# Queue orders from a list scheduler in a fused attention and feed-forward kernel

## The chip, the cores and the metric

The kernel runs on one core of a Trainium2 chip. The metric is the time of one execution on the device in microseconds, as the median of several runs.

## What is computed

Attention over 8 batches, 8 heads, 576 positions and head dimension 64, with a relative-position bias, and then a feed-forward layer over the 4608 rows of 512 that come out of it. Cut to what matters:

```python
scores = matmul(q, k.T) / sqrt(64)                 # 8 x 8 x 576 x 576
n = abs(i - j)                                     # distance of positions
bucket = n if n < 16 else min(31, 16 + int(log(n / 16) / log(8) * 15))
scores += bias_table[bucket, head]                 # constant for n >= 128
attn = exp(scores - max); attn /= attn.sum(-1)
x = matmul(attn, v)                                # as 4608 x 512, heads side by side
h = x @ w_in                                       # 512 -> 2048
out = maximum(0.01 * h, h) @ w_out                 # 2048 -> 512, float32
```

The inputs are float32; the kernel works in bf16 with float32 sums.

## The kernel before

**Attention.** The work is cut into 32 pairs of heads, pair n being batch n // 4 and heads 2p and 2p + 1. For each pair DVE copies the pair's rows of q and k into `pr` (L256), which are transposed to `qt` and `kt`: on PE (L272) with copies out of PSUM (L286, L291) for pairs 0 to 9, by a DMA transpose (L264) from pair 10 on. `apart` (L278) multiplies the last 64 columns with a mask `own`, so that both heads share one matmul there. `qk_mm` (L301 to L309) makes the scores in six chunks, keys along the partitions, into a PSUM pool of two buffers; ACT takes the exponential of each chunk into `at` and `at4` (L319, L321, L326), of which there are two sets, taken in turn. `band` (L347) multiplies the part near the diagonal by the exponentials of the bias, relative to the constant far value, which drops out in the normalization. `av` (L360, L362) makes the product with v for one head (25 matmuls into `ps_o`, one buffer); a column of ones in v gives the sums, and DVE normalizes into `opair` (L365, L366). `x_transposes` brings the pair into `xT`, on PE (L384) with a copy (L385) for pairs 0 to 5 and 31, by DMA (L377) for the others.

**The band factors.** One row of exponentials per head, `ub`, is made by ACT from the transposed table (L183) and by DVE's copies of runs of equal buckets (L186 to L194), stored to a tensor `u_row` in memory (L200), and read back with a shift of one element per partition as `hk` (L202, heads 0 and 1 first) and, for the last 64 keys, `hk4` (L209, `hk_101` in the profile).

**Feed-forward.** Nine tiles of 512 rows. First layer: 16 pieces of 4 matmuls (L396), each followed by ACT's leaky ReLU into `gt` (two buffers). Second layer: 4 row blocks of 16 matmuls (L407), in pieces of 4, each block copied by DVE and stored by SP. All PSUM tiles of these pieces, and of PE transposes, share a pool of three buffers.

**Loads.** q, k, v and the weights are read as float32 and cast on the way, all issued on POOL's queue (software DMA): q and k in `load_qk` (L111), v in L119 to L146, the weights in L232 and L238, in the order of the program.

**What sets the order.** The program is written in the order in which each engine is to run it; every engine takes its own instructions in that order and waits for semaphores. A loop over the pairs holds, for pair n, scores and exponentials in three groups of two chunks, the two AV halves of pair n - 1 between them, the transposes of pair n + 1, and eight slots for feed-forward pieces, alternately of the first and of the second layer:

```python
        moe(1)
        if live:
            exp_band(n, 1, ps_b)
        if n > 0:
            av(n - 1, 0)
        if n + 1 < N:
            transpose_q(n + 1)
```

A piece is taken if its inputs are there by the program's order: a tile of the first layer needs all four pairs of the last batch that it reads, and a tile of the second layer begins only while a tile of the first layer is under way, apart from the end. Junk matmuls (`spin`, L459; 27 of them) fill PE's waits at the start. In batch 0 the band products of pair 0 stand behind its last exponential.

Of the kernel before, what the change touches and what calls it, by code (L numbers as in the profile page):

```python
# [35 lines left out]

@with_exitstack
def kernel(
# [32 lines left out]
    qt_pool = ctx.enter_context(tc.tile_pool(name="qt", bufs=2))  # L71
# [13 lines left out]
    nc.scalar.activation(warm, warm, AF.Exp)  # L85
# [14 lines left out]
    kts_ = [per.tile([P, S + P], BF16, name=f"kt{i}") for i in range(2)]  # L100
# [56 lines left out]
    def clear_edges(eng, i):  # L157
        eng.memset(at_[i][:, ATW : ATW + SL], 1.0)
        eng.memset(at4_[i][:, S : S + SL], 1.0)

    junk = per.tile([P, 512], BF16, name="junk")
    nc.vector.memset(junk, 0.0)
    clear_v(nc.vector, 0)
    clear_edges(nc.vector, 0)
# [3 lines left out]
    tabT = per.tile([H, NB], FP32, name="tabT")  # L168
    with nc.allow_non_contiguous_dma(reason="a table of 256 numbers"):
        nc.sync.dma_start(out=tabT, in_=bias_table.rearrange("u h -> h u"))  # L170
    load_qk(0, 0, 2)
    make_identity(nc, ident)

    e8 = per.tile([H, NB], BF16, name="e8")
    UW = 4 * P
    BW = 3 * P
    ub = per.tile([H, UW], BF16, name="ub")
    nc.vector.memset(ub, 1.0)  # L180
    negc = per.tile([H, 1], FP32, name="negc")
    nc.vector.tensor_scalar(negc, tabT[:, NB - 1 : NB], -1.0, None, op0=ALU.mult)
    nc.scalar.activation(e8, tabT, AF.Exp, bias=negc[:, 0:1], scale=1.0)  # L183
    C0 = 2 * P - 1
    small = NB // 2
    nc.vector.tensor_copy(out=ub[:, C0 : C0 + small], in_=e8[:, 0:small])  # L186
    for u, lo, hi in bucket_runs(NB, BAND, S):
        if lo >= small:
            nc.vector.tensor_copy(
                out=ub[:, C0 + lo : C0 + hi + 1],  # L190
                in_=e8[:, u : u + 1].to_broadcast([H, hi - lo + 1]),
            )
    row = ub[:, :]
    nc.vector.tensor_copy(  # L194
        out=ub[:, C0 - BAND + 1 : C0],
        in_=bass.AP(tensor=row.tensor, offset=row.offset + C0 + BAND - 1,
                    ap=[list(row.ap[0]), [-1, BAND - 1]]),
    )
    udr = nc.dram_tensor("u_row", [H, UW], BF16, kind="Internal")
    nc.sync.dma_start(out=udr.ap(), in_=ub)  # L200
# [6 lines left out]
    load_hk(0, 2)  # L207
    for e in range(2):
        nc.sync.dma_start(  # L209
            out=hk4[e * SL : (e + 1) * SL, :, :],  # L210
            in_=bass.AP(tensor=udr, offset=e * UW + SL + P, ap=[[1, SL], [2 * UW, n_pairs], [1, P + SL]]),
        )
    load_hk(2, H)
# [8 lines left out]

    load_qk(0, 2, H)
    clear_edges(nc.vector, 1)
    load_v(0, 0, 2, True)
    load_v(0, 2, H, False)
    clear_v(nc.gpsimd, 1)
    load_qk(1, 0, H)
# [16 lines left out]
    qts, kts, ops_ = {}, {}, {}  # L245
    N = len(items)
    AHEAD = 3

    prs, turned = {}, {}

    def pair_rows(n):

        b, p = items[n]
        t = prs[n] = pr_pool.tile([RQ, 2, NC, 2 * D], BF16, name="pr")
        for j, src in enumerate((qn, kn)):
            nc.vector.tensor_copy(out=t[:, j, :, :].rearrange("r c (e d) -> r c e d", e=2),  # L256
                                  in_=src[b % NBUF][0:RQ, 2 * p : 2 * p + 2, :, :].rearrange("r e c d -> r c e d"))

    def by_dma(n):
        return n >= 2 * n_pairs + 2  # L260

# [4 lines left out]
    def turned_pair(n, j):  # L266

        if by_dma(n):
            return turned[n][:, j * NC : (j + 1) * NC, :].rearrange("p c r -> p r c")
        ps = ps_m_pool.tile([P, 8 * P], BF16, name="ps_t", tag="m")  # L270
        for c in range(NC):
            nc.tensor.transpose(ps[:, c * RQ : (c + 1) * RQ], in_=prs[n][0:RQ, j, c, :],  # L272
                                identity=ident[0:RQ, 0:RQ])
        return ps[:, 0:S].rearrange("p (c r) -> p r c", c=NC)

    def apart(t):

        nc.vector.tensor_tensor(  # L278
            out=t[:, S : S + P].rearrange("p (e i) -> p e i", e=2),
            in0=t[:, NJ * P : S].unsqueeze(1).to_broadcast([P, 2, SL]),  # L280
            in1=own, op=ALU.mult)

    def transpose_q(n):
        qt = qts[n] = qt_pool.tile([P, S + P], BF16, name="qt")
        copy = nc.scalar.copy if 0 < n < n_pairs else nc.vector.tensor_copy
        copy(out=qt[:, 0:S].rearrange("p (r c) -> p r c", c=NC), in_=turned_pair(n, 0))  # L286
        apart(qt)

    def transpose_k(n):
        kt = kts[n] = kts_[n % 2]  # L290
        nc.vector.tensor_copy(out=kt[:, 0:S].rearrange("p (r c) -> p r c", c=NC), in_=turned_pair(n, 1))  # L291
        apart(kt)

    def qk_mm(n, u):

        qt, kt = qts[n], kts[n]
        ps = ps_s_pool.tile([P, 2, 512], FP32, name="ps_s")
# [12 lines left out]
        return ps  # L310

    def at_view(n):
        return at_[n % 2][:, 0:ATW].rearrange("p (e c i) -> p e c i", e=2, c=NJ)

    def exp_band(n, u, ps):
        b, p = items[n]
        at, at4 = at_view(n), at4_[n % 2]
# [9 lines left out]
        if n > 0:  # L327
            band(n, u)
        elif u == NJ + 1:
            for j in range(NJ + 2):  # L330
                band(n, j)

    def band(n, u):
        b, p = items[n]
        at, at4 = at_view(n), at4_[n % 2]
        hp = hk[:, 2 * p : 2 * p + 2, :]
        if u == 0:
            o, m = at[:, :, 0, 0 : 2 * P], mirrored(hp, P, 3 * P)
        elif u in (1, 2):
            o, m = at[:, :, u, (u - 1) * P : (u + 2) * P], mirrored(hp, 0, 3 * P)  # L340
        elif u == NJ:
            o, m = at[:, :, 3, 2 * P : S], mirrored(hp, 0, S - 2 * P)
        elif u == NJ + 1:
            o, m = at4[:, 3 * P : S], mirrored(hk4[:, p, :], 0, P + SL)
        else:
            return
        nc.vector.tensor_tensor(out=o, in0=o, in1=m, op=ALU.mult)  # L347

    def av(n, e):
        b, p = items[n]  # L350
        i = b % NBUF
        at, at4 = at_[n % 2], at4_[n % 2]
        if e == 0:
            ops_[n] = op_pool.tile([P, NJ + 1, 2 * D], BF16, name="opair")
        opair = ops_[n]
        ps = ps_o_pool.tile([P, NJ + 1, D + 1], FP32, name="ps_o", tag="ps_o")
        for ic in range(NJ + 1):
            for c in range(NJ):
# [4 lines left out]
                             start=False, stop=True)  # L363
        rcp = rc_pool.tile([P, NJ + 1, 1], FP32, name="rcp")
        nc.vector.reciprocal(rcp, ps[:, :, D : D + 1])  # L365
        nc.vector.tensor_tensor(out=opair[:, :, e * D : (e + 1) * D], in0=ps[:, :, 0:D],  # L366
                                in1=rcp.to_broadcast([P, NJ + 1, D]), op=ALU.mult)

    def x_by_dma(n):
        return n_pairs + 2 <= n < N - 1  # L370

    def x_transposes(n):
        b, p = items[n]
        opair = ops_[n]
        w = (NJ + 1) * P
        if x_by_dma(n):
            nc.sync.dma_start_transpose(  # L377
                out=xT[p][:, b * S : b * S + w].rearrange("p (i t) -> p i t", t=P),
                in_=opair.rearrange("p i d -> p (i d)"),
            )  # L380
            return
        ps = ps_m_pool.tile([P, 8 * P], BF16, name="ps_tx", tag="m")
        for ic in range(NJ + 1):
            nc.tensor.transpose(ps[:, ic * P : (ic + 1) * P], in_=opair[:, ic, :], identity=ident)  # L384
        nc.vector.tensor_copy(out=xT[p][:, b * S : (b + 1) * S], in_=ps[:, 0:S])  # L385


    gts = {}

    def ffn_in(T):  # L390
        t0 = T * TT
        gt = gts[T] = gt_pool.tile([P, n_fc, TT], BF16, name="gt")
        for f in range(n_fc):
            pm = ps_m_pool.tile([P, TT], FP32, name="pm1", tag="m")
            for c in range(n_cc):
                nc.tensor.matmul(pm, lhsT=w_in_sb[:, c, f * P : (f + 1) * P], rhs=xT[c][:, t0 : t0 + TT],  # L396
                                 start=(c == 0), stop=(c == n_cc - 1))
            nc.scalar.activation(gt[:, f, :], pm, AF.Prelu, bias=0.0, scale=1.0, alpha=0.01)  # L398
            yield

    def ffn_out(T):
        t0 = T * TT
        gt = gts.pop(T)
        for ts in range(TT // P):
            pm = ps_m_pool.tile([P, DM], FP32, name="pm2", tag="m")
            for f in range(n_fc):
                nc.tensor.matmul(pm, lhsT=gt[:, f, ts * P : (ts + 1) * P], rhs=w_out_sb[:, f, :],  # L407
                                 start=(f == 0), stop=(f == n_fc - 1))
                if f % 4 == 3 and f < n_fc - 1:
                    yield  # L410
# [33 lines left out]
    def moe_rest():  # L444
        while piece("in", True) | piece("out", True):
            pass
# [110 lines left out]
```

## Time and profile before

| | us |
|---|---|
| three runs | 399.03, 397.37, 397.79 |
| median | 397.79 |
| span of the profiled execution, first to last instruction | 396.8 |
| PE busy / ACT busy / DVE busy / POOL busy in it | 372.0 / 247.9 / 203.7 / 66.7 |

The profile is of one execution; for it only the span is given, no separate time, and what lies around the span is in the runs' times alone. Times in its rows count from the start of the span. Busy times of PE overlap from one matmul to the next, so the starts of matmuls tell the rate.

### The profile page before, as it was taken

What the parts mean: (1) busy time and instruction counts of PE and PEld (TensorE: products, weight loads), DVE (VectorE), ACT (ScalarE), POOL (GpSimd) and SP (SyncE); (2) the same over time, 40 slices, a digit from 0 to 9 for tenths busy, and PEclk for the clock granted to TensorE, in tenths of its full rate; (3) what the DMA queues carried; (4) which work ended last, traced back from release to release, by engine and by line L of the source; (5) the groups of instructions that cost most, each with busy time, mean ns of one, the idle gap of its engine ahead of it and who ended that gap; (6) DMA issues with size and microseconds to landing.
All of it is one profiled execution on the core that took longest, in us unless ns stands there. A gap on an engine that the chain in (4) does not pass through costs nothing.

```text
span 396.8 us, 8116 instructions
## 1 busy us (share of the span) xinstructions
PE 372.0 (94%) x3328; PEld 189.9 (48%) x3382; DVE 203.7 (51%) x552; ACT 247.9 (62%) x342; POOL 66.7 (17%) x96
## 2 busy tenths in 40 slices
PE   7678798889999999999999999999999999999995
PEld 3355455444445555554455545554454544444442
DVE  6479778665566666665555665555554310101021
ACT  2677788877777777777777777777777333333300
POOL 8733520340051004200330022000000000000000
PEclk9979999999999999999999999999999999999999
DMA  8999999499279935992599349333111110101112
GB/s 109 194 206 187 203 185 133 64 170 149 68 82 142 165 74 78 158 158 69 64 162 150 70 82 126 74 74 74 43 45 45 43 55 26 55 27 41 40 53 79
DMA packets 103549, 39.89 MB, mean 101 GB/s; under 512 B 82512, under 2 KB 97880, under 8 KB 103512
## 3 DMA queue, kind: packets, MB, share of 16 engines
q0 software_dynamic: 53600, 18.36, 44.6%
q1 hardware_dynamic: 49912, 21.02, 26.2%
q8 instruction: 26, 0.43, 0.5%
q14 instruction: 11, 0.09, 0.1%
HBM read 37.68 MB, written 9.45 MB: 119 GB/s over the span
## 4 chain that ended last, share of the span: by engine, by line
PE 82%; ACT 5%; DVE 5%; DMA 3%; issue 3%; SPq 0%; ACTq 0%; DVEq 0%
PE ps_o L360 8%; PE ps_s L301 7%; ACT at_114 L319 2%; PE ps_o L362 2%; DMA hk<-u_row 2%; ACT at_113 L319 2%; PE ps_s L308 2%; PE ps_s L305 1%; DMA u_row<-ub 1%; DVE opair L366 1%; ACT gt L398 1%; PE pm_4269 L407 1%; PE pm_2498 L407 1%; PE pm_4886 L407 1%; PE pm_3385 L407 1%
## 5 line engine op out<-in xcount | busy, mean ns | idle before, releaser
L396 PEld LDWEIGHTS <-w_in_sb 128*128 128x128 bf16 x576 | 50.1, 98 | 71.9 <-issue 20.1
L407 PEld LDWEIGHTS <-gt 128*128 128x128 bf16 x576 | 53.2, 98 | 56.9
L319 ACT ACTIVATE at_113<-ps_s 128x1024 bf16<-128x1024 f32 x64 | 64.5, 1023 | 17.2 <-PE ps_s L301 16.9
L319 ACT ACTIVATE at_114<-ps_s 128x1024 bf16<-128x1024 f32 x64 | 64.3, 1023 | 11.5 <-PE ps_s L301 11.5
L347 DVE TENSOR_TENSOR at_113<-at_113,hk 128x512 bf16<-128x512 bf16 (+1 forms) x64 | 32.0, 504 | 42.9 <-ACT at_113 L319 40.4
L347 DVE TENSOR_TENSOR at_114<-at_114,hk 128x512 bf16<-128x512 bf16 (+1 forms) x64 | 32.2, 505 | 42.5 <-ACT at_114 L319 41.3
L360 PEld LDWEIGHTS <-at_113 128*128 128x128 bf16 x640 | 27.8, 99 | 13.8 <-DVE opair L366 7.5
L366 DVE TENSOR_TENSOR opair<-ps_o,rcp 128x320 bf16<-128x320 f32 x64 | 31.5, 491 | 2.2
L360 PEld LDWEIGHTS <-at_114 128*128 128x128 bf16 x640 | 27.2, 98 | 9.8 <-DVE opair L366 5.1
L119 POOL DMA_DIRECT2D vn_107<-in_v_dram x12 | 10.6, 897 | 83.3 <-PE ps_o L362 83.3
L301 PE MATMUL ps_s<-qt,kt_111 64*128 64x512 bf16 x128 | 20.9, 389 | 2.7 <-ACT at_114 L319 1.0
L119 POOL DMA_DIRECT2D vn_106<-in_v_dram x12 | 10.8, 911 | 69.2 <-PE ps_o L362 62.7
L301 PE MATMUL ps_s<-qt,kt_110 64*128 64x512 bf16 x128 | 20.3, 382 | 2.0 <-ACT at_113 L319 1.1
L360 PE MATMUL ps_o<-vn_106,at_113 128*128 128x65 bf16 x320 | 15.5, 197 | 4.8 <-DVE opair L366 3.2
L360 PE MATMUL ps_o<-vn_106,at_114 128*128 128x65 bf16 x320 | 14.4, 194 | 1.7 <-DVE opair L366 1.7
L362 PEld LDWEIGHTS <-at_0_115 128*128 128x128 bf16 x160 | 15.7, 98 | 0.0
L362 PEld LDWEIGHTS <-at_1_116 128*128 128x128 bf16 x160 | 15.6, 97 | 0.0
L365 DVE RECIPROCAL rcp<-ps_o 128x5 f32<-128x5 f32 x64 | 12.1, 189 | 6.1 <-PE ps_o L362 6.1
L321 ACT ACTIVATE at_114<-ps_s 128x512 bf16<-128x512 f32 x16 | 9.6, 598 | 8.6 <-PE ps_s L305 8.6
L360 PE MATMUL ps_o<-vn_107,at_113 128*128 128x65 bf16 x320 | 14.3, 193 | 0.1
L360 PE MATMUL ps_o<-vn_107,at_114 128*128 128x65 bf16 x320 | 14.3, 194 | 0.0
L286 DVE COPY qt<-tu 128x576 bf16<-128x576 bf16 x22 | 14.3, 648 | 0.0
(849 smaller groups left out, 760.9 us busy)
## 6 DMA issues: line engine op xcount, KB each, us to landing
out_dram<-y SPq DMA_DIRECT2D x36, 256.0 KB, 2.2
w_in_sb<-in_moe_w_in_dram POOLq DMA_DIRECT2D x2, 1024.0 KB, 13.8
vn_107<-in_v_dram POOLq DMA_DIRECT2D x16, 128.0 KB, 5.2
w_out_sb<-in_moe_w_out_dram POOLq DMA_DIRECT2D x2, 1024.0 KB, 14.2
qn_102<-in_q_dram POOLq DMA_DIRECT2D x6, 288.0 KB, 10.4
kn_104<-in_k_dram POOLq DMA_DIRECT2D x6, 288.0 KB, 10.6
qn_103<-in_q_dram POOLq DMA_DIRECT2D x6, 288.0 KB, 10.6
kn_105<-in_k_dram POOLq DMA_DIRECT2D x6, 288.0 KB, 11.2
```

Source lines behind the costliest of these rows:

```text
L119: nc.gpsimd.dma_start(out=vn[i][:, c, :, 0:D], in_=v[b, :, c * P : (c + 1) * P, :].rearrange("h s d -> s h d"),)
L286: copy(out=qt[:, 0:S].rearrange("p (r c) -> p r c", c=NC), in_=turned_pair(n, 0))
L301: nc.tensor.matmul(ps[:, e, :], lhsT=kt[r, u * P : (u + 1) * P], rhs=qt[r, 0:512], start=True, stop=True)
L319: nc.scalar.activation(at[:, :, u, 0:512], ps, AF.Exp, scale=scale)
L321: nc.scalar.activation(at[:, :, :, 512:S].rearrange("p e c i -> p c e i"), ps[:, 0, :].rearrange("p (c e i) -> p c e i", e=2, i=SL), AF.Ex ...
L347: nc.vector.tensor_tensor(out=o, in0=o, in1=m, op=ALU.mult)
L360: nc.tensor.matmul(ps[:, ic, :], lhsT=at[:, o : o + P], rhs=vn[i][:, c, 2 * p + e, :], start=(c == 0), stop=False)
L362: nc.tensor.matmul(ps[:, ic, :], lhsT=at4[:, ic * P : (ic + 1) * P], rhs=v4[i][:, p, e, :], start=False, stop=True)
L365: nc.vector.reciprocal(rcp, ps[:, :, D : D + 1])
L366: nc.vector.tensor_tensor(out=opair[:, :, e * D : (e + 1) * D], in0=ps[:, :, 0:D], in1=rcp.to_broadcast([P, NJ + 1, D]), op=ALU.mult)
L396: nc.tensor.matmul(pm, lhsT=w_in_sb[:, c, f * P : (f + 1) * P], rhs=xT[c][:, t0 : t0 + TT], start=(c == 0), stop=(c == n_cc - 1))
L407: nc.tensor.matmul(pm, lhsT=gt[:, f, ts * P : (ts + 1) * P], rhs=w_out_sb[:, f, :], start=(f == 0), stop=(f == n_fc - 1))
```

## The change

The loop is replaced by a plan. Each step of the program becomes a task with an engine, a cost in us that is written into the code, the tasks it comes after, the PSUM buffers it takes and gives back, and a rank. At build time `Plan.order` simulates the engines: again and again it takes the task that can start first, ties going to the lower rank, and the program is emitted in that order. Attention has ranks 10 n, feed-forward 10000 and up, so a feed-forward piece is taken where no attention task is ready. Batch 0's scores get rank 10 n - 25 and come ahead of AV. Loads have landing times written in. From pair 8 on, scores also wait for a first-layer piece (`PACE`, `LEAD`), so that attention does not run too far ahead. Junk matmuls fill the planned waits of PE ahead of the first feed-forward piece; they are again 27.

Other edits: `qt` and `kt` have three buffers instead of two; pair 2's exponentials go to a third attention buffer, which lies in the second `gt` buffer until tile 1 needs it. q and k of pair 0 are read as float32 without a cast on SP's and ACT's queues into the first `gt` buffer (`raw`), and cast by DVE (q) and ACT (k) in the row copies; all of batch 0's v likewise by six DMAs on ACT's queue, cast by POOL. The band row is a matmul of the exponentials of the table (32 buckets x 8 heads) with a one-hot matrix `hot` that DVE builds from the identity; one DVE copy brings it to `ub`. The order of the read-backs is now hk of heads 0 and 1, hk of heads 2 to 7, hk4. POOL's loads are held by `gate`, a one-element copy that waits: the last q and k load of batch 0 until `ub` exists, the first half of `w_in` until hk of heads 2 to 7 has landed. Behind it follow q and k of batch 1 (first half), the second half of `w_in`, v of batch 1, the rest of q and k, and `w_out`. The masks for v and the edges are cleared by POOL. Products with `own` of pairs 1 and 2 go to POOL; the copies into `qt` of pairs 0 to 2 and 4, and into `kt` of pair 4, to ACT. Pair 0's band products come as soon as the factors are there. In batch 0 the second AV half uses a buffer of the shared pool in place of `ps_o`. Pair 7's output is transposed by PE, not by DMA. The second layer of a tile may begin whenever its first layer is complete.

```diff
+class Plan:
...
+    def order(self):
...
+                for t in ts:
+                    if any(d["end"] is None for d in t["after"] + t["behind"]):
+                        continue
+                    r = now
+                    for d in t["after"]:
+                        r = max(r, d["end"] + (self.LAG if d["engine"] != e else 0.0))
+                    for k in set(t["take"]):
+                        s, m = sorted(self.slots[k]), t["take"].count(k)
+                        r = max(r, s[m - 1]) if len(s) >= m else None
...
+                    key = (r, t["rank"], t["n"])
+                    if pick is None or key < pick[0]:
+                        pick = (key, t, r)
...
-    qt_pool = ctx.enter_context(tc.tile_pool(name="qt", bufs=2))
+    qt_pool = ctx.enter_context(tc.tile_pool(name="qt", bufs=3))
...
+    nc.sync.dma_start(out=raw[:, 0, :, :], in_=q[0, 0:2, :, :].rearrange("h (r c) d -> r h (c d)", c=NC))
+    nc.scalar.dma_start(out=raw[:, 1, :, :], in_=k[0, 0:2, :, :].rearrange("h (r c) d -> r h (c d)", c=NC))
+    nc.sync.dma_start(out=tab[:, 0, :], in_=bias_table)
...
+    load_qk(0, 2, 4)
+    load_qk(0, 4, 6)
...
+    def spread_table():
+        ps = outs["u"] = ps_o_pool.tile([P, 512], FP32, name="ps_u", tag="ps_o")
+        nc.tensor.matmul(ps[0:H, :], lhsT=e8, rhs=hot, start=True, stop=True)
...
+    def load_v_raw():
+        for c in range(NJ):
+            nc.scalar.dma_start(out=vraw_sb[:, c, :, :], in_=v[0, :, c * P : (c + 1) * P, :].rearrange("h s d -> s h d"))
+        for e in range(2):
+            nc.scalar.dma_start(out=vraw4[e * SL : (e + 1) * SL, :, :],
+                                in_=v[0, e::2, NJ * P : S, :].rearrange("h s d -> s h d"))
...
+    def gate(t):
+        nc.gpsimd.tensor_copy(out=w_in_sb[0:1, 0, 0:1], in_=t)
...
+    plan = Plan({"S": 2, "O": 1, "M": 2})
...
+    e8t = add("ACT", 0.25, [sh], exp_table, -1)
+    spr = add("PE", 0.4, [e8t], spread_table, -1, take=["O"])
+    cpu = add("DVE", 0.6, [spr], copy_u_row, -1, give=["O"])
+    urt = add("SP", 0.1, [cpu], store_u_row, -1, tail=2.6)
+    hkt = add("SP", 0.1, [urt], lambda: load_hk(0, 2), -1, tail=2.8)
+    hkr = add("SP", 0.1, [urt], lambda: (load_hk(2, H), load_hk4()), 1, tail=5.5)
...
+    pool_load(("qk", 0, 2), 1.6, lambda: (gate(ub[0:1, 0:1]), load_qk(0, 6, H)), after=[cpu], land=17.0)
+    vrt = add("ACT", 0.6, [], load_v_raw, 5, tail=9.0)
+    vc = [add("POOL", 0.7, [vrt], lambda c=c: cast_v(c), 0) for c in range(NJ + 1)]
...
+            t = add("PE", 0.3 * len(us), ds + before + order_s[-1:],
+                    lambda us=us: [score(n, u) for u in us], rank + (-25 if n < n_pairs else 2), take=["S"] * len(us))
...
+        for e in range(2):
+            k = "M" if b == 0 and e == 1 else "O"
+            avs.append(add("PE", 0.78, done, lambda e=e: av(n, e), soon + 4, take=[k]))
+            nms.append(add("DVE", 0.68, [avs[-1]] + old + nms, lambda e=e: norm(n, e), soon + 3, give=[k]))
...
-    for n in range(N + 1):
...
-    moe_rest()
+    spin(9)
+    plan.run(spin)
```

In the order that results, PE's queue for batch 0 is: junk, the one-hot matmul, the transposes of pair 0, then scores of pair 0 and 1 with the transposes of pairs 1 and 2; the first AV half of pair 0 stands between score chunks 2 and 3 of pair 1, its second half between chunks 3 and 4. The first feed-forward piece stands behind score chunk 1 of pair 4, and the second layer of tile 0 begins among the pairs of batch 1. From batch 2 on each pair has eight feed-forward pieces, as before.

More of the change, by code (lines that the diff above doesn't have):

```diff
@@ L182 @@
[L182 to L198, printed above, removed]
-    udr = nc.dram_tensor("u_row", [H, UW], BF16, kind="Internal")
-    nc.sync.dma_start(out=udr.ap(), in_=ub)
+    clear_v(nc.gpsimd, 0)
+    for i in range(3):
+        clear_edges(nc.gpsimd, i)
+    clear_v(nc.gpsimd, 1)
+    e8 = per.tile([NB, H], BF16, name="e8")
@@ L367, in av, with x_dma @@
                                 in1=rcp.to_broadcast([P, NJ + 1, D]), op=ALU.mult)
-    def x_by_dma(n):
-        return n_pairs + 2 <= n < N - 1
-    def x_transposes(n):
+    def x_dma(n):
         b, p = items[n]
-        opair = ops_[n]
         w = (NJ + 1) * P
-        if x_by_dma(n):
[L377 to L385, printed above, removed]
@@ L401, in ffn_out @@
-    def ffn_out(T):
-        t0 = T * TT
-        gt = gts.pop(T)
-        for ts in range(TT // P):
[L405 to L410, printed above, removed]
-            y = y_pool.tile([P, DM], FP32, name="y")
-            nc.vector.tensor_copy(out=y, in_=pm)
-            nc.sync.dma_start(out=out[t0 + ts * P : t0 + (ts + 1) * P, :], in_=y)
-            yield
```

528 lines of the change are left out of this document (338 added, 190 removed).

## The prediction

> **What bounds the kernel now.** I read the page first (span, the 40 slices), then cut the span into stages with the table by windows, then followed the first stage in the timeline and in the chain that ended last.
>
> ```profile
> span 396.8 us, 8116 instructions
> PE   7678798889999999999999999999999999999995
> DMA  8999999499279935992599349333111110101112
> ```
> ```profile
> 0.00:44.00 44.00, 32.03 (x389) 18.86 (x392) 30.92 (x106) 27.94 (x36) 24.17 (x40) 0.92 1.33 177
> 44.00:84.60 40.60, 34.96 (x438) 20.03 (x445) 30.34 (x83) 32.57 (x46) 15.29 (x21) 1.00 1.23 142
> 84.60:314.00 229.40, 226.70 (x2123) 114.88 (x2159) 131.58 (x348) 165.25 (x224) 27.21 (x36) 1.00 0.72 99
> 314.00:396.80 82.80, 78.27 (x382) 36.09 (x388) 10.84 (x17) 22.10 (x37) 0.00 (x0) 1.00 0.12 45
> ```
>
> In the windows the columns are length, then busy time of PE, PEld, DVE, ACT and POOL, granted clock, DMA share, GB/s. From 84.6 us to the end PE is the limit: 2.70 us idle of 229.40. Nothing but less PE work could shorten that part, and the change takes none away. Idle time lies ahead of it: 11.97 us in the first 44, 5.64 in the next 40.6. At the later rate (2.70 in 229.40) 40.6 us would have 0.48 idle, so 5.2 us of excess lie there. What the change can be worth is therefore two numbers: the moment S at which the feed-forward part can begin, and the excess after it.
>
> ```profile
> 0.74 1.28 ACT L85 ACT_TABLE_LOAD   x1 [0.74 <-PEq L541]
> 2.04 0.20 ACT L85 ACTIVATE warm<-warm 128x1 f32<-128x1 f32 x1
> 3.44 0.32 ACT L183 ACTIVATE e_136<-tabT,negc 8x32 bf16<-8x32 f32 x1 [1.20 <-DVE negc L182]
> 5.53 0.28 SPq L200 DMA_DIRECT2D u_row<-ub  x1
> 8.92 1.94 ACT L319 ACTIVATE at_113<-ps_s 128x1024 bf16<-128x1024 f32 x2 [5.16 <-PE ps_s L301]
> 11.45 1.34 SPq L209 DMA_DIRECT2D hk_101<-u_row  x2
> 12.83 0.61 SPq L202 DMA_DIRECT2D hk<-u_row  x1
> 16.45 1.76 DVE L347 TENSOR_TENSOR at_113<-at_113,hk 128x512 bf16<-128x512 bf16 x4 [2.28 <-DMA hk<-u_row]
> 31.88 3.77 ACT L319 ACTIVATE at_114<-ps_s 128x1024 bf16<-128x1024 f32 x4 [0.20 <-PE ps_s L301]
> 43.96 0.38 PE L396 MATMUL pm_774<-xT_95,w_in_sb 128*128 128x512 bf16 x1
> ```
> ```profile
> 5.53 5.46 DMA u_row<-ub
> 12.83 7.37 DMA hk<-u_row
> ```
>
> The first exponentials start at 8.92, but the band factors arrive only at 16.45: the row is stored in 5.46 us and read back until 16.45. The pairs then follow one another, and S is 44.0. From S to the end of the span are 396.8 - 44.0 = 352.8 us.
>
> **Part 1, the start.** Scores of pair 0 need its q and k, whose first copies now wait in ACT's queue behind seven DMA issues (one for k, six for v). SP's issues above took 0.28, 0.67 (half of 1.34) and 0.61 us; ACT's own issues are not in the trace, so the bounds are 0.28 and 0.67 each. The v transfers have the larger shape, so I take 0.6. ACT: 0.74 + 0.4 (k) + 1.28 (table) + 0.2 + 6 x 0.6 = 6.2, then the exponential of the table, 0.3. The one-hot matmul (0.38, as the 512-column matmul above) and its copy out of PSUM (0.7, by the copies of 576 columns below) give the band row at 7.6 us, 2.1 later than in the profile (with 0.28 an issue: 5.7). Behind the same ACT issues stand ACT's copy of k (0.8, from 0.65 for 576 columns), six transposes (0.42), DVE's 0.75 copy and the score: 7.3, 7.7, 8.5, first exponential at 8.9, as now. The fp32 loads save nothing that ACT's queue does not take back.
>
> ```profile
> 26.65 0.42 PE L272 MATMUL ps_t<-ident,pr 96*128 96x96 bf16 x6
> L291 DVE COPY kt_111<-ps_t 128x576 bf16<-128x576 bf16 x5 | 3.7, 749 | 0.4 <-PE ps_t L272 0.4
> out_dram<-y SPq DMA_DIRECT2D x36, 256.0 KB, 2.2
> w_in_sb<-in_moe_w_in_dram POOLq DMA_DIRECT2D x2, 1024.0 KB, 13.8
> ```
>
> Store and first read-back took 16.45 - 5.53 = 10.9 us together. The lower bound is two undisturbed transfers, 2 x 2.2 = 4.4. The gate holds the next q/k load back until the row exists, but the six v loads are in flight, so I take the middle, 7.5: band factors at 15.1 (bounds 10.1 and 18.5). The Trainium skill (DMA: Bandwidth & Descriptors, "Issuing engines are not separate DMA queues") says that loads from different queues run on the same 16 DMA engines and interleave. By that rule v on ACT's queue gets no lane of its own and the upper bound would hold. The profile agrees as far as it goes: DMA is at 9 in the second to seventh slice.
>
> **Part 2, batch 0.** Third buffer and hoisted scores let ACT run on while the factors are missing. ACT's chain: first exponential 8.9, four pairs of 3.77 + 0.60 + 0.64, two q copies of 0.65 between: 8.9 + 20.0 + 1.3 = 30.2.
>
> ```profile
> 10.75 0.65 ACT L286 COPY qt<-ps_t 128x576 bf16<-128x576 bf16 x1
> L321 ACT ACTIVATE at_113<-ps_s 128x512 bf16<-128x512 f32 x16 | 9.6, 598 | 6.8 <-PE ps_s L305 6.8
> L326 ACT ACTIVATE at_0_115<-ps_s 128x576 bf16<-128x576 f32 x16 | 10.3, 644 | 0.0
> L365 DVE RECIPROCAL rcp<-ps_o 128x5 f32<-128x5 f32 x64 | 12.1, 189 | 6.1 <-PE ps_o L362 6.1
> L366 DVE TENSOR_TENSOR opair<-ps_o,rcp 128x320 bf16<-128x320 f32 x64 | 31.5, 491 | 2.2
> L347 DVE TENSOR_TENSOR at_114<-at_114,hk 128x512 bf16<-128x512 bf16 (+1 forms) x64 | 32.2, 505 | 42.5 <-ACT at_114 L319 41.3
> L347 DVE TENSOR_TENSOR at_0_115<-at_0_115,hk_101 128x192 bf16<-128x192 bf16 x16 | 4.1, 257 | 9.7 <-ACT at_0_115 L326 9.7
> L256 DVE COPY pr<-kn_104 96x768 bf16<-96x768 bf16 x16 | 6.0, 372 | 2.5 <-DMA kn_104<-in_k_dram 2.5
> L278 DVE TENSOR_TENSOR kt_110<-kt_110,own 128x128 bf16<-128x128 bf16 x16 | 3.6, 225 | 0.5
> L385 DVE COPY xT_94<-ps_tx x2: 452/455/458, 25.4 to 53.2; 128x576 bf16<-128x576 bf16 x2
> ```
>
> But nothing of a pair can finish before its factors, and DVE then has it all. Counted in the new instruction order from the first band product to the last xT copy of batch 0: 16 products of 0.505 and 4 of 0.257 (9.1), 8 normalizations of 0.189 + 0.491 (5.4), 6 row copies of 0.372 (2.2), 4 xT copies of 0.455 (1.8), 2 copies of 0.749 (1.5), 4 products with own of 0.225 (0.9): 20.9 us. At the end DVE waits for the last pair's AV (0.76, below) and transposes (0.45), of which I count 1.5 with hops. So S = 15.1 + 20.9 + 1.5 = 37.5. By ACT alone it would be 30.2 + 0.26 + 2 x 0.76 + 0.68 + 0.45 + 0.45 = 33.6. The bounds of S are 33.6 (row early, ACT decides) and 18.5 + 22.4 = 40.9.
>
> Two waits are new there. In PE's queue the first AV stands ahead of score chunk 3 of pair 1; behind it queue the scores that feed ACT. That AV also needs the narrow factors hk_101, which SP now issues last, behind the large hk load that took 7.37: at about 19.5, where ACT would need the score at 18.1 (8.9 + 5.0 + 1.3 + three chunks). With product, AV and score (0.26, 0.76, 0.3) ACT stands 2.7 us, and the S of ACT's chain is 36.3, still under DVE's. On POOL the gates stand ahead of the last q/k load of batch 0, the casts of v, the products with own of pairs 1 and 2 (needed by chunks 4 and 5 only) and the first half of w_in. w_in starts when the factors of the other heads are in, at 19 to 20, and lands within 13.8: 33 to 34, covered by 3.5 us; if the factors come that much later, w_in is the last to come. The order of the later loads (q/k, w_in, v, w_out) costs nothing as long as PE has first-layer pieces.
>
> **Part 3, after S.** More work is left at S than before: four of pair 4's six score chunks (0.27 each by the rows below, 1.1), pair 5's 12 transposes (0.84) and pair 7's output transpose on PE (0.45): 2.4 us. Against it, second-layer pieces may now run before the next tile's first layer begins; in the profile the first one ran at 84.6. Of the 5.2 excess I take back 3.7 (bounds 0 and 5.2), since w_out still lands late in that stage. The attention steps now stand in PE's queue as early as the planned times allow.
>
> ```profile
> L407 PE MATMUL pm_2498<-w_out_sb,gt x16: 377/379/382, 155.9 to 164.6; 128*128 128x512 bf16 x16
> L407 PE MATMUL pm_4269<-w_out_sb,gt x16: 377/379/382, 278.2 to 286.8; 128*128 128x512 bf16 x16
> 382.33 3.45 PE pm_5209 L407 x16
> 158.61 0.60 PE L301 MATMUL ps_s<-qt,kt_111 64*128 64x512 bf16 x4
> 160.02 0.28 PE L360 MATMUL ps_o<-vn_106,at_113 128*128 128x65 bf16 x4
> 160.78 1.03 PE L407 MATMUL pm_2498<-w_out_sb,gt 128*128 128x512 bf16 x4
> 29.03 0.30 PE L360 MATMUL ps_o<-vn_106,at_114 128*128 128x65 bf16 x4 [0.84 <-DVE opair L366]
> ```
>
> A pair takes 122.3 / 12 = 10.19 us there, of which eight pieces of 3.45 / 4 = 0.86 are 6.9 and attention 3.3; an AV half is 160.78 - 160.02 = 0.76. The new order has the same pieces. Between the two AV halves of a pair, which share one ps_o, it leaves mostly two score chunks and one piece (about 1.4 us), where the steady loop now leaves 3.1. The normalization between them is 0.68 and a hop, so it fits if DVE is free; where it was not, PE waited 0.84. Bounds over 28 pairs: 0 and 23.5. DVE is busy 131.58 of 229.40, mostly with short steps, so I take 0.5. What the new order gives the steady part is nothing: PE was full.
>
> **The sum.** Span: 37.5 + 352.8 + 2.4 - 3.7 + 0.5 = 389.5. The profiled execution's 396.8 stands 1.0 under the median of the runs, 397.79; with that, **390.5 us**. With the skill's rule on shared engines S would be 40.9 and the time 393.9.
>
> **Rivals.**
> 1. Band factors as slow as now: S 40.9, time 393.9. For it: full DMA slices, v's loads moved into this very stage. Against: fewer bytes are queued at 7.6 us than at 5.53 before.
> 2. The start gives nothing: ACT's issues last until v has drained, or w_in is last. From S = 42.8 on the time is within 0.5% of 397.79 (what a measurement here can tell from no change); at S = 43 it is 396.
> 3. Slower: the short distance between AV halves makes PE wait for the normalization in every pair. From 0.26 us a pair the gain of 7.3 is gone, from 0.33 it is over 0.5% slower; at half of 0.84 it is 28 x 0.42 = 11.8 in place of my 0.5: 401.8. For it: greedy times leave no slack, and such waits add up over 28 pairs. Against: second-layer pieces need no new buffer and stand between.
> 4. Early: factors at 10 to 11, S 33.6 to 34, all 5.2 back, no waits: 34.0 + 352.8 + 2.4 - 5.2 + 1.0 = 385.0.
>
> That the plan changes nothing is excluded by the new order: the first feed-forward pieces stand behind pair 4's second score chunk, the second layer's ahead of batch 2's.
>
> **Chances.** Forecast 0.50, rival 1 0.13, rival 4 0.12 (faster, 0.75); rival 2 0.10 (same); rival 3 0.15 (slower). The forecast's own range, S 36 to 39.5 and 1 us of steady waits either way, is 388 to 393.5. To hold 8 in 10 the range takes in rivals 1, 2 and 4, whose low end is 385 less half a microsecond, and the mild end of rival 3: 384.5 to 399.
>
> **What would show it.** The band row stored near 7.6, first band product near 15, first feed-forward matmul near 37.5; DVE without gaps in between; PE idle under 2.5 us in the 40 us after S; 10.2 us a pair from then on. Wrong if the pair takes over 10.5 (rival 3), if the first feed-forward matmul waits for w_in, or if S is over 42.

## The result, and the profile after

The changed kernel took 407.66 us (median of four runs, 406.33 to 408.00) beside 397.58 for the kernel before on the same chip (397.06 to 399.03): ratio 1.0232, 95% interval 1.0202 to 1.0261. It is 2.3% slower. The forecast was 390.5 with a range of 384.5 to 399.0, so both the sign and the range were wrong.

The page of the changed kernel, the rows that answer to those shown of before:

```profile
span 406.1 us, 8302 instructions
PE   3898906999999999999999999999999999999995
PEclk8699975999999999999999999999999999999999
DMA  9759999833995994898399399111111010010112
```

Slices six and seven hold the news: TensorE at 0 and 6, its clock at 7 and 5, with DMA at 9. The windows of the same run, cut at the first feed-forward matmul and around that hole (columns as in the prediction):

```profile
0.00:41.70 41.70, 30.94 (x368) 17.14 (x368) 27.64 (x87) 24.84 (x34) 21.86 (x49) 0.88 0.93 160
50.50:64.20 13.70, 0.12 (x5) 0.01 (x1) 1.97 (x6) 1.54 (x2) 3.74 (x5) 0.69 1.37 200
64.20:70.00 5.80, 5.80 (x49) 3.25 (x49) 2.48 (x9) 1.19 (x2) 1.50 (x2) 0.55 1.98 140
84.60:314.00 229.40, 229.40 (x2290) 117.58 (x2287) 144.00 (x380) 170.20 (x236) 35.20 (x46) 1.00 0.75 102
```

The steady part is full: 229.40 busy of 229.40, where the kernel before had 226.70. The time went in one hole, 13.58 us without a matmul, and in the 5.8 us behind it at a granted clock of 0.55, worth another 5.8 x 0.45 = 2.6 us. Without these 16.2 us the run would have been near the forecast. The timeline around the hole, first VectorE's rows, then TensorE's, then GpSimd's issues:

```profile
61.41 0.61 DVE L383 COPY pr<-qn 96x768 bf16<-96x768 bf16 x1 [15.08 <-DMA qn<-in_q_dram]
62.85 0.36 DVE L383 COPY pr<-kn 96x768 bf16<-96x768 bf16 x1 [0.82 <-DMA kn<-in_k_dram]
63.66 0.65 DVE L463 TENSOR_TENSOR at<-at,hk 128x640 bf16<-128x640 bf16 x2
64.19 0.24 PE L478 MATMUL ps_o<-vn,at 128*128 128x65 bf16 x1 [13.58 <-DVE at L463]
44.05 0.88 POOL L355 DMA_DIRECT2D w_out_sb<-in_moe_w_out_dram  x1 [0.27 <-DMA vn<-in_v_dram]
46.11 0.69 POOL L193 DMA_DIRECT2D qn<-in_q_dram  x1 [1.18 <-DMA vn<-in_v_dram]
47.47 0.67 POOL L193 DMA_DIRECT2D kn<-in_k_dram  x1 [0.67 <-DMA v<-in_v_dram]
```

Read it from the bottom. The q and k of pairs 8 and 9, the first half of batch 2, are issued at 46.11 and 47.47, behind both halves of w_out, and land some 15 us later. VectorE's queue holds the row copies of these pairs ahead of the last two band products of pair 4. From 46.3 on VectorE waits for that data, although pair 4's last exponentials are there at 49; TensorE waits for the product, and nothing behind these instructions can overtake them.

The scheduler had taken batch 2's landing as the end of the issue plus 11 us, at an issue time of its own clock. `Plan.order` of the changed kernel, worked out from its code, has this load issued at 26.75 and landed at 39.25. The trace has 46.11 and 61.4: of 22 us of error 19 lie in the issue. Where these come from shows in the chain of work that ended last (some of its pieces; start, length, what):

```profile
10.83 0.62 ACTq L312
23.76 0.40 POOL w_in_sb L337
24.45 8.27 DMA w_in_sb<-in_moe_w_in_dram
33.00 14.40 DMA v<-in_v_dram
47.47 15.35 DMA kn<-in_k_dram
```

The last of v's issues on ScalarE's queue ends at 11.45. Through the late row, the casts and the gate, the first half of w_in is issued only at 24.45, where the plan has 14.65, and everything behind it in GpSimd's queue is late with it; there the next issues also wait for earlier transfers, 4.26 us ahead of the one at 41.76. So the late start and the hole are one chain.

### The profile page after: what moved, and what is told of

Read it like the earlier page. It is cut to its first block, busy times and chain, and to the rows that moved or that the text cites. A ratio compares the mean times of both kernels' runs of the same rounds, so it can differ in the third digit from the quotient of the medians.

```text
span 406.1 us, 8302 instructions
## 1 busy us (share of the span) xinstructions
PE 377.5 (93%) x3388; PEld 191.5 (47%) x3388; DVE 203.8 (50%) x539; ACT 243.2 (60%) x345; POOL 69.8 (17%) x112
## 3 DMA queue, kind: packets, MB, share of 16 engines
q0 software_dynamic: 48512, 17.47, 39.8%
## 4 chain that ended last, share of the span: by engine, by line
PE 84%; DMA 9%; ACTq 2%; POOL 2%; issue 1%; DVE 1%; ACT 1%; POOLq 0%
PE pm L533 31%; PE pm L521 30%; PE ps_o L478 9%; PE ps_s L430 7%; DMA kn<-in_k_dram 4%; DMA v<-in_v_dram 4%; PE ps_o L480 2%; DMA w_in_sb<-in_moe_w_in_dram 2%; PE ps_s L434 1%; PE ps_s L437 1%; ACTq L312 1%; PE ps_t L393 1%; POOL vn L331 1%; ACTq L310 1%; PE ps_w L710 0%
## 5 line engine op out<-in xcount | busy, mean ns | idle before, releaser
L521 PE MATMUL pm<-xT,w_in_sb 128*128 128x512 bf16 x576 | 147.2, 383 | 0.0
L533 PE MATMUL pm<-w_out_sb,gt 128*128 128x512 bf16 x576 | 144.3, 379 | 0.0
L526 ACT ACTIVATE gt<-pm 128x512 bf16<-128x512 f32 x144 | 86.1, 601 | 92.2 <-PE pm L521 90.9
L444 ACT ACTIVATE at<-ps_s 128x1024 bf16<-128x1024 f32 x124 | 120.1, 1024 | 27.0 <-PE ps_s L430 26.4
L463 DVE TENSOR_TENSOR at<-at,hk 128x768 bf16<-128x768 bf16 (+3 forms) x155 | 69.4, 461 | 22.1 <-ACT at L444 17.2
L478 PEld LDWEIGHTS <-at 128*128 128x128 bf16 x1240 | 52.7, 98 | 31.0 <-DVE at L463 16.7
L538 DVE COPY y<-pm 128x512 f32<-128x512 f32 x36 | 24.8, 690 | 83.8 <-PE pm L533 83.4
L478 PE MATMUL ps_o<-vn,at 128*128 128x65 bf16 x1180 | 54.0, 195 | 13.6 <-DVE at L463 13.6
L480 PE MATMUL ps_o<-v,at 128*128 128x65 bf16 x295 | 47.9, 195 | 0.2 <-POOL v L334 0.2
L430 PE MATMUL ps_s<-qt,kt 64*128 64x512 bf16 x256 | 40.9, 388 | 1.2 <-ACT at L446 0.5
L480 PEld LDWEIGHTS <-at 128*128 128x128 bf16 x310 | 30.4, 98 | 0.0
```

Of the source, the lines that this page charges most:

```text
L430: nc.tensor.matmul(ps[:, e, :], lhsT=kt[r, u * P : (u + 1) * P], rhs=qt[r, 0:512], start=True, stop=True)
L444: nc.scalar.activation(at[:, :, u, 0:512], ps, AF.Exp, scale=scale)
L478: nc.tensor.matmul(ps[:, ic, :], lhsT=at[:, o : o + P], rhs=vn[i][:, c, 2 * p + e, :], start=(c == 0), stop=False)
L480: nc.tensor.matmul(ps[:, ic, :], lhsT=at4[:, ic * P : (ic + 1) * P], rhs=v4[i][:, p, e, :], start=False, stop=True)
L521: nc.tensor.matmul(pm[:, j * w : (j + 1) * w], lhsT=w_in_sb[:, c, f * P : (f + 1) * P], rhs=xT[c][:, t0 : t0 + w], start=(c == 0), stop=(c ...
L526: nc.scalar.activation(gts[T][:, f0 : f0 + TT // w, 0:w], pms.pop((T, f0)).rearrange("p (j t) -> p j t", t=w), AF.Prelu, bias=0.0, scale=1 ...
```

## The experiments

All ratios are to the kernel before, on the same chip.

**Telling the scheduler when batch 2 lands.** On the changed kernel, two landing times change. GpSimd's order stays, so no transfer changes its place in the queue; the eight row copies of pairs 8 to 11 go behind band products, and the order behind them follows.

```diff
             L["qk", b, hh] = add("POOL", 1.5, ...)
+            if b == 2:
+                L["qk", b, hh]["land"] = 62.0 + 2.0 * hh
```

> The changed kernel, and the only edit tells the scheduler that the q and k of batch 2 land at 62 and 64 us, as the profile of the changed kernel shows, where it had taken issue plus 11 us. That puts VectorE's row copies of pairs 8 and 9 behind the band products of pair 4; no transfer moves. Theory A (the row copies, queued ahead of band products, held VectorE, and through it everything, for 15 us): the gap of 13.6 us ahead of pair 4's AV half goes, 392 to 395 us. Rival B (TensorE would have been short of data there anyway, since v of batch 1, w_out and batch 2 all arrive between 33 and 63 us): the stretch from 50 to 63 us stays mostly empty, 404 to 407 us.

Measured: 391.12 us, a little under theory A's 392 to 395, ratio 0.9818 (0.9797 to 0.9840). Its span is 389.5. The window of the former hole:

```profile
50.50:64.20 13.70, 13.52 (x166) 7.93 (x165) 10.26 (x29) 11.54 (x17) 3.03 (x5) 1.00 1.39 200
```

VectorE's first copy for pair 8 in its timeline, now without a wait, and the feed-forward matmuls as a group (count, shortest, median and longest in ns, then the first and last start):

```profile
66.84 0.35 DVE L383 COPY pr<-qn 96x768 bf16<-96x768 bf16 x1
```
```profile
L521 PE MATMUL pm<-xT,w_in_sb x61: 377/379/389, 41.4 to 64.6; 128*128 128x512 bf16 x61
```

The hole is gone, and 16.5 us with it: the whole loss and the gain that it hid. DMA moved the same 200 GB/s in that stretch, so TensorE had not been short of data. Rival B falls.

**The start: v by GpSimd again.** Batch 0's v is loaded by GpSimd's converting transfers in place of the six fp32 transfers on ScalarE's queue, alone and then together with the landing times.

```diff
+    vt[0] = add("POOL", 5.0, [], lambda: load_v(0, 0, H, False), 0, tail=9.0)
-    vrt = add("ACT", 0.6, [], load_v_raw, 5, tail=9.0)
-    vc = [add("POOL", 0.7, [vrt], lambda c=c: cast_v(c), 0) ...]
```

> The changed kernel with batch 0's v loaded as before the change, by GpSimd's converting transfers, in place of the six fp32 transfers on ScalarE's queue with GpSimd casts behind them; everything else of the change stays. Theory A (the six transfers on ScalarE's queue hold ScalarE for about 10 us, so that the first exponential comes at 15.3 us): the first exponential at about 9 us, first band product at 14 to 16 in place of 19.9, the first feed-forward matmul 4 to 6 us earlier than 41.7. The 13.6 us gap behind it depends on the landing of batch 2 and stays, perhaps longer by what TensorE is early: 403 to 408 us. Rival B (the start is bounded by the landing of the small table and of q and k, not by ScalarE's queue): first band product after 18 us and no earlier first feed-forward matmul.

> Both edits together: batch 0's v by GpSimd's converting transfers, and the scheduler told that batch 2's q and k land at 62 and 64 us. Theory A (two separate losses, 15 us of VectorE held by queued row copies and 4 to 6 us of ScalarE held by its transfers): 386 to 391 us, faster than the kernel before by 2 to 3%. If the start is made good but TensorE is then short of data (rival B): no better than the run with the landing times alone.

Measured: 401.38 us alone (ratio 1.008, 1.005 to 1.011), below the 403 to 408 expected and 6.3 less than the changed kernel; 391.55 with the landing times (0.9829, 0.9787 to 0.9872), no better than the landing times alone. What held ScalarE shows in the changed kernel's own timeline (its queue's issues, then its first instructions, then SyncE's store of the row and the first band product), and in the group of feed-forward matmuls:

```profile
1.29 3.71 ACTq L310 DMA_DIRECT2D first<-in_v_dram  x3
5.03 1.43 ACTq L310 DMA_DIRECT2D first<-in_v_dram  x1
6.50 4.95 ACTq L312 DMA_DIRECT2D first<-in_v_dram  x2
11.49 0.21 ACT L296 ACTIVATE e<-tab 32x8 bf16<-32x8 f32 x1 [8.78 <-issue]
15.27 1.94 ACT L444 ACTIVATE at<-ps_s 128x1024 bf16<-128x1024 f32 x2 [1.67 <-PE ps_s L430]
13.08 0.33 SPq L306 DMA_DIRECT2D u_row<-ub  x1
19.89 4.21 DVE L463 TENSOR_TENSOR at<-at,hk 128x512 bf16<-128x512 bf16 x7
```
```profile
L521 PE MATMUL pm<-xT,w_in_sb x29: 377/379/616, 41.7 to 64.8; 128*128 128x512 bf16 x29
```

Six issues took 10.1 us. With v on GpSimd's queue and without the landing times, the first feed-forward matmul comes 4.0 us earlier and the hole is 3.0 us shorter, since GpSimd issues batch 2's q at 38.89 in place of 46.11:

```profile
L521 PE MATMUL pm<-xT,w_in_sb x33: 376/379/634, 37.7 to 64.9; 128*128 128x512 bf16 x33
54.96 0.36 DVE L383 COPY pr<-qn 96x768 bf16<-96x768 bf16 x1 [11.98 <-DMA qn<-in_q_dram]
57.50 0.24 PE L478 MATMUL ps_o<-vn,at 128*128 128x65 bf16 x1 [10.55 <-DVE at L463]
```

With v on GpSimd's queue and the landing times told, these are the answering rows:

```profile
6.29 0.21 ACT L296 ACTIVATE e<-tab 32x8 bf16<-32x8 f32 x1 [3.60 <-DVE tab L293]
9.24 1.94 ACT L444 ACTIVATE at<-ps_s 128x1024 bf16<-128x1024 f32 x2 [1.28 <-PE ps_s L430]
14.14 2.30 DVE L463 TENSOR_TENSOR at<-at,hk 128x512 bf16<-128x512 bf16 x4 [0.57 <-ACT qt L405]
19.29 0.59 DVE L463 TENSOR_TENSOR at<-at,hk 128x192 bf16<-128x192 bf16 x2 [2.85 <-DMA hk<-u_row]
19.84 0.22 PE L478 MATMUL ps_o<-vn,at 128*128 128x65 bf16 x1 [1.80 <-DMA vn<-in_v_dram]
```
```profile
L521 PE MATMUL pm<-xT,w_in_sb x60: 376/379/390, 39.8 to 64.7; 128*128 128x512 bf16 x60
```

ScalarE starts 6 us earlier, but VectorE then waits until 19.29 for the narrow factors and TensorE until 19.84 for v, so of 5.8 us at the first band product 1.9 are left at the first feed-forward matmul (41.7 to 39.8). In the run without the landing times, whose order is the same up to there, v was there at 18.31 and 4.0 us were left: two executions of one start differ by 2 us. Theory A was right on ScalarE, and on the gain where it stands alone; with the landing times the medians show none. One possible reason was left untested: the times told stayed at 62 and 64, although q was issued at 40.10 here.

**Two issues on ScalarE's queue.** On top of the landing times, only the first two of the six v transfers stay there; GpSimd loads the rest.

```diff
     def load_v_raw():
-        for c in range(NJ):
+        for c in range(2):       # chunks 2, 3 and the last 64 rows by GpSimd
```

> The run with batch 2's landing times told to the scheduler, in which only the first two of the six v transfers of batch 0 stay on ScalarE's queue (fp32, cast by GpSimd); the other four go through GpSimd's converting transfers. In the changed kernel the first two issues on ScalarE's queue took 0.61 and 0.35 us and the four behind them 9.1. Theory A (only the issues from the third on hold ScalarE): exponential of the table at about 6 us in place of 11.2, first band product at 14 to 15, v complete at 17 to 19, first feed-forward matmul at 38 to 40. By the runs so far an earlier first feed-forward matmul brings little by itself (39.8 against 41.4: no difference): 388 to 391.5 us. Rival (ScalarE is held by any transfer of this kind until it has drained): exponential of the table at 8 us or later, no change against 391.1.

Measured: 390.68 us, ratio 0.9819 (0.9796 to 0.9841).

```profile
1.27 1.06 ACTq L317 DMA_DIRECT2D first<-in_v_dram  x2
7.07 0.21 ACT L296 ACTIVATE e<-tab 32x8 bf16<-32x8 f32 x1 [4.37 <-DVE tab L293]
```
```profile
L525 PE MATMUL pm<-xT,w_in_sb x60: 376/379/390, 37.2 to 62.1; 128*128 128x512 bf16 x60
```

Two issues cost 1.06 us; ScalarE then waits for the table. The first band product came at 16.29, a little late. The first feed-forward matmul comes at 37.2, and the profiled execution took 388.26, but the other three 390.24 to 391.35: the median is not to be told from that of the landing times alone. It is the lowest median of all, and both are 1.8% faster than the kernel before.

**Other edits of the start.** Pair 2's q and k loaded behind v; no gate on the factors ahead of w_in (both on top of the run with both edits); two attention buffers in place of three (on top of the landing times).

```diff
-    load_qk(0, 4, 6)                      # pair 2: issued behind load_v instead
-    ... lambda: (gate(hk[0:1, H - 1, 0:1]), load_w_in(0)), after=[hkr]
+    ... lambda: load_w_in(0)              # no gate
-        if n == 2: return spare           # two buffers: at_buf(n) is n % 2
```

> The run with both edits, and GpSimd's loads of pair 2's q and k moved behind v's. In that run v landed at 19.8 and the rest of the factors at 19.3, so VectorE, which had its first band product at 14.1, stood still until 22. Theory A (the start is bounded by bytes: v and the factors share the transfers with pair 2's q and k, some 576 KB or 3 us at 190 GB/s): v and factors at about 17, first feed-forward matmul at 36 to 38 in place of 39.8, 387 to 390 us. Rival (what the start gains is taken back by the loads behind it, w_in and batch 2, as in the run with both edits): 390 to 393 us.

> The run with both edits, without the gate that holds the first half of w_in until the factors of the other heads have landed. Theory A (in the first 20 us the bytes bound the start): w_in's first MB delays v, the factors or pair 3's q and k by up to 5 us, first feed-forward matmul at 40 to 45, 391 to 396 us. Rival (the gate leaves transfers idle that the later loads need; without it w_in, v of batch 1 and batch 2 land 4 to 6 us earlier): 387 to 390 us.

> The run with batch 2's landing times told to the scheduler, with two attention buffers in place of three (pair n waits for pair n-2 throughout batch 0); the rest stays. Theory A (ahead of the first feed-forward matmul VectorE's queue decides, so that the hoisted scores of the third buffer only help as long as VectorE waits for the factors): first feed-forward matmul at 41 to 43, 391 to 394 us. Rival (the third buffer carries the gain of batch 0): first feed-forward matmul at 44 or later, 395 to 399 us.

Measured: 393.37 (ratio 0.9888, 0.9855 to 0.9923), 393.22 (0.9876, 0.9850 to 0.9902) and 391.50 us (0.9831, 0.9809 to 0.9853). First feed-forward matmuls of the three, in that order:

```profile
L520 PE MATMUL pm<-xT,w_in_sb x46: 376/379/390, 46.7 to 64.9; 128*128 128x512 bf16 x46
```
```profile
L521 PE MATMUL pm<-xT,w_in_sb x61: 376/379/389, 40.7 to 64.9; 128*128 128x512 bf16 x61
```
```profile
L519 PE MATMUL pm<-xT,w_in_sb x62: 377/379/390, 42.2 to 64.9; 128*128 128x512 bf16 x62
```

Loading pair 2 later was a miss: its feed-forward part began at 46.7. Taking the gate away gains nothing (393.22 against 391.55, with intervals that overlap). The third buffer and the scores hoisted into it bring nothing that a run can tell (391.50 against 391.12).

The medians hide what the start is worth. Taken from one and the same execution, the span less the first feed-forward matmul is 348.1 with the landing times alone, 349.4 with v on GpSimd's queue, 349.3 with two issues, and 347.1, 349.7 and 348.0 in the three runs here: 9.5 us in the start (37.2 to 46.7) are 7.3 in the span (386.5 to 393.8). That the other executions of these kernels began at the same moments is not shown.

**Less to wait for, or another queue to wait in.** On the changed kernel as it is: w_out behind batch 2's q and k; the row copies of pairs 8 and 9 on GpSimd; those of pairs 8 to 11.

```diff
-    pool_load(("w_out", 0), ...); pool_load(("w_out", 1), ...)   # moved behind load_qk(2, ...)
     def rows_by_pool(n):
-        return False
+        return n in (8, 9)                # the third run: (8, 9, 10, 11)
```

> The changed kernel with the two w_out transfers issued behind batch 2's q and k instead of ahead of them; the landing times that the scheduler is told stay as in the changed kernel, so VectorE's row copies of pairs 8 and 9 stay ahead of the bands of pair 4. Theory A (the gap is the wait of those row copies for batch 2's q and k, which were queued behind w_out): q lands 10 to 13 us earlier, the gap of 13.6 us shrinks to under 4 us, 394 to 399 us unless the first second-layer matmuls then wait for w_out. Rival B (short of data in any order): 404 to 408 us.

> The changed kernel, in which only the four row copies of pairs 8 and 9 go from VectorE's queue to GpSimd's; the transfers, their order and the rest of VectorE's order stay. The copies still wait for batch 2's q and k, which land as late as before (about 61 to 63 us). Theory A (what cost the 15 us is that these copies stood in VectorE's queue ahead of band products, not the late data): 390 to 394 us, the gap ahead of pair 4's AV half gone. Rival B (pairs 8 and 9, or TensorE, need that data then in any case): 403 to 408 us.

> As the run with the row copies of pairs 8 and 9 on GpSimd, and those of pairs 10 and 11 as well. That run ended the wait at 46 to 61 us, but VectorE then stood from 58.7 to 63.9 in front of the next copy of the same kind, pair 10's, and TensorE was nearly empty from 62 to 68. Theory A (each such copy holds whatever queue it stands in): without any of batch 2's copies in VectorE's queue the second gap goes too, 391 to 395 us, unless TensorE's own transposes of pairs 8 and 9, which stand in its queue at the same planned times, hold TensorE instead (then the gap stays, with the copies on GpSimd as its releaser: 398 to 402). Rival B (short of data): the gap stays with DMA as its releaser, 399 to 403 us.

Measured: 401.10 (ratio 1.0069, 1.0043 to 1.0094), 401.17 (1.0073, 1.0053 to 1.0093) and 404.63 us (1.0171, 1.0137 to 1.0206). None of the three lies in a range named for it. In the first, q lands 11 us earlier and the hole shrinks to 3.67, as expected, but later copies of the same line wait:

```profile
53.20 0.24 PE L478 MATMUL ps_o<-vn,at 128*128 128x65 bf16 x1 [3.67 <-DVE at L463]
76.25 0.35 DVE L383 COPY pr<-qn 96x768 bf16<-96x768 bf16 x1 [3.81 <-DMA tu<-pr]
81.98 0.35 DVE L383 COPY pr<-qn 96x768 bf16<-96x768 bf16 x1 [4.38 <-DMA tu<-pr]
```

In the second the first hole is gone, and pair 10's copy makes the next (GpSimd's first and last copy of the four, VectorE's copy, the AV):

```profile
63.55 0.84 POOL L383 COPY pr<-qn 96x768 bf16<-96x768 bf16 x1
...
65.85 0.83 POOL L383 COPY pr<-kn 96x768 bf16<-96x768 bf16 x1
63.86 3.03 DVE L383 COPY pr<-qn 96x768 bf16<-96x768 bf16 x1 [5.18 <-DMA qn<-in_q_dram]
68.52 0.40 PE L478 MATMUL ps_o<-vn,at 128*128 128x65 bf16 x4 [6.57 <-DVE opair L490]
```

In the third, GpSimd's copy of pair 11 waits 7.44 us for a DMA transpose of rows, and VectorE's next row copy 10.60 for another:

```profile
77.79 0.82 POOL L383 COPY pr<-qn 96x768 bf16<-96x768 bf16 x1 [7.44 <-DMA tu<-pr]
83.13 0.36 DVE L383 COPY pr<-qn 96x768 bf16<-96x768 bf16 x1 [10.60 <-DMA tu<-pr]
```

So my theory in its narrow form, that only the copies ahead of pair 4 did it, is refuted: moving them gave 6.5 of 16.5 us, and moving more gave less. What replaced it (theory C): all queues were written for data that came about 15 us later than the engines reached it, and each entry of batch 2 holds whichever queue it stands in. The next two runs test its first half.

**Other landing times.** The first experiment again with wrong times on either side of the true 62 and 64.

```diff
-                L["qk", b, hh]["land"] = 62.0 + 2.0 * hh
+                L["qk", b, hh]["land"] = 55.0 + 2.0 * hh    # second run: 72.0 + 2.0 * hh
```

> The run with batch 2's landing times told to the scheduler, but told as 55 and 57 us where they are about 62 and 64. Theory C (what costs is that the queues are written for data that comes later: every entry of batch 2 stands that much too early in its in-order queue, and moving some entries to another queue only moves the wait): about half of the error is left, so a wait of 4 to 8 us in VectorE's queue near 57 to 64 us, 395 to 401 us. Theory A in its narrow form (only copies ahead of pair 4's bands hurt): 390 to 393 us.

> As before, told as 72 and 74 us, ten later than they are. Theory C: an entry that stands too late in a queue waits for nothing as long as TensorE has feed-forward pieces to do; batch 2's first scores are only needed when batch 1's pieces run short, so 390 to 393 us, no gap in VectorE over 3 us. Rival (the order must fit the landing from both sides; too late starves the scores and ScalarE): 394 us or more.

Measured: 398.52 us (ratio 1.0021, 0.9996 to 1.0045) and 398.19 (0.9982, 0.9950 to 1.0013; single runs from 394.08 to 400.08, the slowest left out of the ratio). Seven us too early costs 7.4, as theory C has it, though not where I put it: the copies of pairs 8 to 11 wait at most 1.07 us, and those of the loads that follow wait longer. Ten too late costs about 7 in the median: theory C's second half, that late entries are free, is wrong. The longest wait of each (VectorE of the early, ScalarE of the late one):

```profile
77.81 0.36 DVE L383 COPY pr<-kn 96x768 bf16<-96x768 bf16 x1 [4.94 <-DMA kn<-in_k_dram]
```
```profile
82.30 1.94 ACT L444 ACTIVATE at<-ps_s 128x1024 bf16<-128x1024 f32 x2 [7.67 <-PE ps_s L430]
```

With 72 ScalarE has no scores until 82.3, and pairs bunch up behind it. That the execution with this profile was the fastest of ten, and why single runs of this order spread so far, stays open.

## Why the prediction was wrong

- **The step that failed** is Part 2's last sentence, "The order of the later loads (q/k, w_in, v, w_out) costs nothing as long as PE has first-layer pieces." PE had pieces, but they stood in its queue behind an AV that waited for VectorE, and VectorE for q. I counted VectorE's work in the new order and never asked of each entry when its data lands, although the row needed stood in the prediction: a transfer of 1024 KB took 13.8 us to land, and the new order issues two of them, w_out's, right ahead of batch 2's q and k (in the kernel before, batch 2's were issued from 31.65 to 35.11 and w_out from 35.77 on). No rival had this mechanism. It cost 16.5 us, by the run with the landing times alone. Part of the lateness came from the next point: with v off ScalarE's queue the hole was 10.55 in place of 13.58.
- **Part 1** had the right queue and the wrong size. The bounds of 0.28 and 0.67 us an issue, from SyncE's small transfers, left out that an issue can wait: the first two v issues fit them (1.06 together in the later run), six took 10.1. Row stored at 13.08, not 7.6; first exponential 15.27, not 8.9; first band product 19.89, where I had the factors between 10.1 and 18.5. From the store to that product it took 6.8 us, where I had 7.5 for store and read-back, and the product stood behind a copy of k in VectorE's queue, so the factors were there no later; the term mis-sized was the issues. This was rival 2's mechanism. Its price was less than the rival's: S 41.7 where it said 43.
- **Part 2's sum** held: 19.89 + 20.9 + 1.5 = 42.3 for a first feed-forward matmul at 41.7. It was also not held by w_in, whose first half landed at 32.7.
- **Part 3** was too cautious. From S to the end I had 352.8 + 2.4 - 3.7 + 0.5 = 352.0; in the run with the landing times it is 389.5 - 41.4 = 348.1. The start came 3.9 later than forecast (41.4, 37.5), the rest was 3.9 shorter, and so that run's span equals the forecast 389.5: two errors that cancel, no confirmation. The pairs also run otherwise than Part 3 and the section on the change have it: for most pairs of batches 2 to 5 the new order has six feed-forward pieces, not eight, and from 117.75 to 186.28 a pair takes 8.6 us in place of 10.2; eight pieces and 10.2 us come from 231 on.
- **Rival 3** is refuted: TensorE is busy throughout the steady part. So the short distance of the AV halves costs nothing there.
- **The rule on shared engines** (the Trainium skill, DMA: Bandwidth & Descriptors, "Issuing engines are not separate DMA queues") is not put to the test at this place: the row went out at 13.08, and the DMA engines moved only 18, 0 and 14 GB/s in the three slices of 0.6 us from 12.6 on, so v was no longer under way. The 10.9 us that I had by it for store and read-back did not come (at most 6.8).

## What to carry to other kernels

An order written ahead by a scheduler is as good as its landing times. Take each load's issue and landing from a profile, behind the megabytes that are queued ahead of it, and look in every in-order queue for entries whose data lands after the entries behind them could run; moving such an entry to another queue moved much of the wait with it here (6.5 of 16.5 us came back, 3.0 with two more pairs moved). The time of issue was the larger part of the error. And weigh a start against the end of the same execution: medians of four hid it here, with one start that came at 37.7 in one execution and at 39.8 in another.

## What had not been expected of the hardware

- Transfers issued on ScalarE's queue block ScalarE: two of 256 KB take 1.06 us, the six together 10.1, and the exponential behind them waits 8.78.
- After the 13.6 us without matmuls the granted clock was 0.55 over the next 5.8 us, and the first eight feed-forward matmuls behind it took 3.41 us; eight at full clock took 1.83 in the same run (both from the chain that ended last):

```profile
65.03 3.41 PE pm L521 x8
79.37 1.83 PE pm L521 x8
```
  The Trainium skill (TensorE: Matmul & The Clock Gate, "Part 1: The HAM clock gate") says that the array falls to half rate after an idle window of about 3.4 us; the trace agrees.
- A VectorE copy that takes 0.35 us elsewhere took 3.03 beside GpSimd's four copies of rows (above). The Trainium skill (SBUF — State Buffer, "SBUF: two separate sides") says that the two engines can lock each other out of a port pair for a whole instruction. The row agrees that VectorE is held, but it was held for about as long as all four copies together (63.55 to 66.68), and a single one lasted 0.84. No run here tests the lock by itself.
